# Value products of the first attention batch in two groups per pair of heads, instead of five

## Chip, cores, metric

One core of one Trainium2 chip runs the whole program. The metric is the device time of one execution in microseconds; the kernel before has a median of 1145.33 us over 3 runs (1145.01 to 1146.11).

## The reference

Four batches of attention with 8 heads, 576 positions and a head size of 64, followed by two feed-forward layers over the 4 x 576 tokens:

```python
scores = scale * np.matmul(q, k.transpose(0, 1, 3, 2))
thresh = np.max(scores, axis=-1, keepdims=True) - tau
scores = np.where(scores >= thresh, scores, -1000000000.0)
attn = np.exp(scores - np.max(scores, axis=-1, keepdims=True))
attn = attn / (np.sum(attn, axis=-1, keepdims=True) + 1e-09)
x = np.matmul(attn, v)                 # to (2304, 512)
h = x @ w_in;   x = (np.maximum(h, 0.0) + alpha * np.minimum(h, 0.0)) @ w_out
h = x @ w_in2;  y = (h * np.clip(h + 3.0, 0.0, 6.0) / 6.0) @ w_out2
```

## The kernel before

**Attention.** Heads are taken two at a time: 4 batches give 16 pairs (`pairs`, line 281), `NP` = 4 pairs to a batch. A pair has `NT` = 9 steps. Steps 0 to 7 each take 128 queries of one of the two heads, in turn; step 8 takes the last 64 queries of both heads. In a step `do_S` (line 377) makes a tile of scores on TensorE; `soft` takes its maximum on VectorE (L398), the exponential on ScalarE (L399) and the threshold with the sum on VectorE (L401). After each odd step, and after step 8, `soft_norm` divides by the sums on GpSimd (L413), `do_T` transposes the weights of both heads on TensorE (L432, L435) and ScalarE copies them to SBUF (L433, L436), and `do_PV` multiplies by the values. Beside this, `prep` gets the next pair ready in the same steps: loads on SP's queue (L296, L299), a split into a rounded part and a rest (L101 on ScalarE, L102 on GpSimd), transposes on TensorE (L322) and copies on ScalarE (L331, L342).

**The value products.** `do_T` puts the weights of steps 1 and 3 into one tile `p` of two halves, and those of steps 5 and 7 into another; there are two such buffers. Step 8 has a tile `p1` of its own. `do_PV` (lines 440 to 478) forms `pv` in PSUM, from the pool `ps_ho` of two buffers, by 5 blocks of keys for each of 2 heads, so 10 products, and a product is two matmul instructions in the trace. ScalarE copies `pv` to `xo` (L470). In the first batch (`b == 0`) this is done five times in a pair: after steps 1, 3, 5 and 7 for 128 queries, after step 8 for 64. In the other batches it is done twice: after step 3 for 256 queries, after step 8 for 256 and 64 together. After step 8 the result of the pair is split into `x0` for the feed-forward of the first batch (ScalarE L101, GpSimd L102), or stored (L476), and the last 64 rows are stored (L477). The values of the pair after next go to the buffer of this pair's (`vs`, two buffers), so their load stands on SP's queue until step 8's products are done.

**Feed-forward.** Hidden chunks of 128 (`h_group`, L216) and output groups (`o_group`, L245 and L251). The weights arrive in a 64-bit format and are decoded chunk by chunk in the first block (`decode`, L148 to L154); the first ten chunks are loaded and decoded during the first batch of attention, at steps listed in `EARLY`. The feed-forward of a block starts some steps after its attention (`LAG`), mixed into the attention of the next batch by a fixed share per step (`per`).

**Order.** The code is written in the order of the loop at line 589. A scheduler of the framework then orders the instructions of each engine by a simulated timeline, with attention raised in priority (`high_priority`); on the chip each engine runs its own list in that order.

Of the kernel before, what the change touches and what calls it, by code (L numbers as in the profile page):

```python
# [32 lines left out]
def kernel(  # L33
# [22 lines left out]
    NP = H // 2  # L56
# [43 lines left out]
    def split(hi, lo, src, lo_eng):  # L100
        nc.scalar.copy(hi, src)  # L101
        lo_eng.tensor_tensor(out=lo, in0=src, in1=f32(hi), op=ALU.subtract)  # L102
# [337 lines left out]
    def do_PV(i):  # L440
        pi, t = divmod(i, NT)
        b, hp = pairs[pi]
        vn = vs[pi % 2]
        if b == 0:
            parts = [(1, st["p"][1], 0)] if t == NT - 1 else [(2, st["p"][0], t % 4 // 2)]
        elif t in (3, NT - 1):
            parts = [(2, st["p"][0], None)] + [(1, p1, 0) for p1 in st["p"][1:]]
        else:
            return
        pv = ps_ho.tile([P, SM], F32, tag="ho", name="pv")  # L450
        at = 0
        for n, pt, u in parts:
            m = SR if n == 1 else P if u is not None else 2 * P
            for kt in range(NB + 1):
                for h in range(2):
                    blk = n * NB if kt == NB else kt + NB * h * (n - 1)
                    o = pv[64 * h:64 * h + 64, at:at + m]
                    if n == 1:
                        r = pt[:, 0, blk, SR * h:SR * h + m]
                    elif u is None:  # L460
                        o, r = o.rearrange("p (u q) -> p u q", u=2), pt[:, :, blk, :]
                    else:
                        r = pt[:, u, blk, :]
                    nc.tensor.matmul(o, lhsT=vn[:, h, kt, :], rhs=r, start=(kt == 0 and at == 0), stop=(kt == NB), skip_group_check=True)  # L464
            at += m
        if "xo" not in st[pi]:
            st[pi]["xo"] = a2.tile([P, S], F32, tag="xo", name="xo")
        xo = st[pi]["xo"]
        end = S if t == NT - 1 else t // 2 * P + P
        nc.scalar.copy(xo[:, end - at:end], pv[:, 0:at])  # L470
        if t < NT - 1:
            return
        if b == 0:
            split(x0[:, 0, hp], x0[:, 1, hp], xo[:, 0:SM], nc.gpsimd)
        else:
            nc.sync.dma_start(x1d[b][hp], xo[:, 0:SM])  # L476
        nc.sync.dma_start(x1d[rem_blk][hp, :, b * SR:(b + 1) * SR], xo[:, SM:S])  # L477
        del st[pi]
# [110 lines left out]
    for i in range(NS):  # L589
        pi, t = divmod(i, NT)  # L590
        with tc.high_priority(offset=50):
            prep(pi + 1, t)
            do_S(i)
            soft(i)
        if t % 2 == 1 or t == NT - 1:
            with tc.high_priority(offset=50):
                n = 1 + t % 2
                soft_norm(n, i)
                do_T(n, t)
                do_PV(i)  # L600
            if i in EARLY:
                if len(ws) < 7:
                    ready(*EARLY[i])
                at = early.index(EARLY[i]) + 2
                if at < len(early):
                    fetch(*early[at])
        if i % PB == PB - 1:
            emitted.add(i // PB)
        while done < min(len(queue), (i + 1 - PB - LAG) * per):
            f, a = queue[done]  # L610
            f(*a)
            done += 1
# [94 lines left out]
```

## Time and profile before

| | |
|---|---|
| Median of 3 runs | 1145.33 us |
| The profiled execution's own time | 1145.86 us |
| Its span, first to last instruction | 1144.1 us |
| TensorE, mean granted clock | 0.995 |
| TensorE busy | 1109.8 us (97%) |
| ScalarE busy | 692.4 us (61%) |
| Value products (L464), instructions | 1120 |

The engines are PE (TensorE's matmuls), PEld (its weight loads), DVE (VectorE), ACT (ScalarE), POOL (GpSimd) and SP (the queue that issues DMAs). L464 is line 464 of the kernel. A busy time is a sum over instructions and says nothing of who waits; the chain of waits goes back from the last instruction to whatever released each one.

### The profile page before, as it was taken

What the parts mean: (1) busy time and instruction counts of PE and PEld (TensorE: products, weight loads), DVE (VectorE), ACT (ScalarE), POOL (GpSimd) and SP (SyncE); (2) the same over time, 40 slices, a digit from 0 to 9 for tenths busy, and PEclk for the clock granted to TensorE, in tenths of its full rate; (3) what the DMA queues carried; (4) which work ended last, traced back from release to release, by engine and by line L of the source; (5) the groups of instructions that cost most, each with busy time, mean ns of one, the idle gap of its engine ahead of it and who ended that gap; (6) DMA issues with size and microseconds to landing.
All of it is one profiled execution on the core that took longest, in us unless ns stands there. A gap on an engine that the chain in (4) does not pass through costs nothing.

```text
span 1144.1 us, 18508 instructions
## 1 busy us (share of the span) xinstructions
PE 1109.8 (97%) x6464; PEld 913.9 (80%) x6464; DVE 611.9 (53%) x1215; ACT 692.4 (61%) x1316; POOL 681.5 (60%) x726
## 2 busy tenths in 40 slices
PE   6998999998999999999999999999999999999998
PEld 5776787877887888888878788887778888888886
DVE  6879778989897535464545535462334222232121
ACT  6989788888887565566656555565444333343332
POOL 3777779987889755556555756545334333334432
PEclk9999999999999999999999999999999999999999
DMA  5546347666775433333333522322235222222201
GB/s 166 160 130 193 115 154 228 215 217 191 223 204 191 155 107 87 106 96 107 105 101 110 151 91 63 100 72 80 84 99 172 66 65 65 61 61 65 62 31 56
DMA packets 92765, 137.44 MB, mean 120 GB/s; under 512 B 19328, under 2 KB 48512, under 8 KB 92672
## 3 DMA queue, kind: packets, MB, share of 16 engines
q1 hardware_dynamic: 92672, 136.26, 39.8%
q8 instruction: 51, 0.84, 0.3%
q14 instruction: 42, 0.34, 0.1%
HBM read 101.72 MB, written 25.17 MB: 111 GB/s over the span
## 4 chain that ended last, share of the span: by engine, by line
PE 81%; DVE 5%; ACT 4%; issue 4%; POOL 3%; DMA 2%; SPq 0%; DVEq 0%; ACTq 0%; POOLq 0%
PE h L216 32%; PE o L245 14%; PE o L251 13%; PE pv L464 7%; PE s L377 6%; PE t L432 4%; PE r L251 2%; PE r L245 2%; PE pt L322 1%; DVE nmx L398 1%; DVE e L401 1%; DMA st<-wo 1%; POOL nat L102 1%; DVE low L150 1%; POOL gs L241 1%
## 5 line engine op out<-in xcount | busy, mean ns | idle before, releaser
L216 PE MATMUL h<-x,wi 128*128 128x512 f32 (+1 forms) x1536 | 356.8, 381 | 0.0
L216 PEld LDWEIGHTS h<-x,wi 128*128 128x128 f32 x1536 | 271.9, 188 | 54.7 <-issue 1.2
L241 POOL TENSOR_TENSOR gs<-g,gs 128x512 fp32r<-128x512 f32 (+1 forms) x160 | 193.1, 1208 | 163.9 <-ACT gs L237 160.4
L251 PE MATMUL o<-wo,gs 128*128 128x512 f32 x768 | 194.8, 398 | 4.6 <-DVE g L231 2.7
L245 PE MATMUL o<-gs,wo 128*128 128x512 f32 x768 | 194.5, 397 | 0.7 <-DVE g L223 0.3
L251 PEld LDWEIGHTS o<-wo,gs 128*128 128x128 f32 x768 | 140.8, 188 | 37.8 <-DVE g L231 5.6
L245 PEld LDWEIGHTS o<-gs,wo 128*128 128x128 f32 x768 | 140.2, 188 | 30.1 <-DVE g L223 1.4
L399 ACT ACTIVATE e<-s,nmx 128x576 f32<-128x576 f32 x144 | 107.5, 750 | 48.9 <-DVE nmx L398 48.3
L231 DVE SCALAR_TENSOR_TENSOR g<-m,h 128x512 f32<-128x512 f32 x80 | 50.5, 632 | 162.0 <-ACT m L229 158.4
L401 DVE SCALAR_TENSOR_TENSOR e<-s,thr,e 128x576 f32<-128x576 f32 x144 | 116.0, 812 | 35.4 <-ACT e L399 34.8
L223 DVE SCALAR_TENSOR_TENSOR g<-m,rest_sb,h 128x512 f32<-128x512 f32 x80 | 55.3, 691 | 145.3 <-ACT m L221 134.3
L398 DVE TENSOR_REDUCE nmx<-s 128x1 f32<-128x576 f32 x144 | 106.8, 751 | 47.3 <-PE s L377 46.6
L102 POOL TENSOR_TENSOR wi<-st,wi 128x512 fp32r<-128x512 f32 x56 | 72.2, 1289 | 99.5 <-ACT wi L101 99.2
L413 POOL TENSOR_SCALAR e<-e,rc 128x576 f32<-128x576 f32 x144 | 112.5, 792 | 27.7 <-DVE rc L410 26.1
L237 ACT CAST gs<-g 128x512 fp32r<-128x512 f32 (+1 forms) x160 | 93.2, 583 | 34.6 <-DVE g L231 12.0
L229 ACT ACTIVATE m<-h,three 128x512 f32<-128x512 f32 x80 | 51.7, 648 | 102.0 <-PE h L216 102.0
L377 PE MATMUL s<-ka,qt 128*128 128x288 f32 x512 | 98.9, 320 | 6.5 <-DVE thr L400 3.7
L101 ACT CAST wo<-st 128x512 fp32r<-128x512 f32 x96 | 57.2, 620 | 78.1 <-DMA st<-wo 62.6
L221 ACT ACTIVATE m<-h 128x512 f32<-128x512 f32 x80 | 44.4, 555 | 94.0 <-PE h L216 93.5
L102 POOL TENSOR_TENSOR wo<-st,wo 128x512 fp32r<-128x512 f32 x56 | 74.3, 1344 | 41.3 <-ACT wo L101 41.3
L464 PE MATMUL pv<-p,v 128*64 128x256 f32 (+2 forms) x1120 | 97.0, 310 | 1.4 <-ACT p L433 1.1
L433 ACT COPY p<-t 128x512 f32<-128x512 f32 x144 | 82.1, 594 | 23.4 <-PE t L432 14.4
(88 smaller groups left out, 1605.0 us busy)
## 6 DMA issues: line engine op xcount, KB each, us to landing
st<-wi SPq DMA_DIRECT2D x96, 256.0 KB, 2.7
st<-wo SPq DMA_DIRECT2D x96, 256.0 KB, 2.7
raw<-in_moe_w_in_dram SPq DMA_DIRECT2D x32, 512.0 KB, 4.2
raw<-in_moe_w_out_dram SPq DMA_DIRECT2D x32, 512.0 KB, 3.9
ka<-ka SPq DMA_DIRECT2D x30, 304.0 KB, 4.4
wi<-f SPq DMA_DIRECT2D x32, 256.0 KB, 3.2
wo<-f SPq DMA_DIRECT2D x32, 256.0 KB, 3.1
raw<-in_k_dram SPq DMA_DIRECT2D x16, 256.0 KB, 3.7
```

The costliest lines, as they stand in the source:

```text
L102: lo_eng.tensor_tensor(out=lo, in0=src, in1=f32(hi), op=ALU.subtract)
L216: nc.tensor.matmul(h[:, :n], lhsT=w[:, ws, kt * P:(kt + 1) * P], rhs=x[:, xs, kt, :n], start=(i == 0), stop=(i == len(steps) - 1))
L237: nc.scalar.copy(gs[:, 0, :n], g[:, :n])
L241: nc.gpsimd.tensor_tensor(out=gs[:, 1, :n], in0=g[:, :n], in1=f32(gs[:, 0, :n]), op=ALU.subtract)
L245: nc.tensor.matmul(o[:, :n], lhsT=w[:, ws, dt * P:(dt + 1) * P], rhs=gs[:, gsel, :n], start=fresh and start and i == 0, stop=stop and i == ...
L251: nc.tensor.matmul(o[:m, :], lhsT=gs[:, gsel, tt * P:tt * P + m], rhs=w[:, ws, :], start=start and i == 0, stop=stop and i == 2)
L377: nc.tensor.matmul(ps[:, half, 0:SH], lhsT=w, rhs=s["k"][:, a, c + half * SH:c + half * SH + SH], start=(n == 0), stop=(n == len(mms) - 1))
L398: nc.vector.tensor_reduce(out=nmx, in_=ps, axis=AX.XY, op=ALU.max, negate=True)
L399: nc.scalar.activation(eh, ps, AF.Exp, bias=nmx, scale=1.0)
L401: nc.vector.scalar_tensor_tensor(out=eh, in0=ps, scalar=thr, in1=eh, op0=ALU.is_ge, op1=ALU.mult, accum_out=sm[:, h:h + 1])
L413: nc.gpsimd.tensor_scalar(out=eh, in0=eh, scalar1=rc[:, h:h + 1], scalar2=0.0, op0=ALU.mult, op1=ALU.add)
L464: nc.tensor.matmul(o, lhsT=vn[:, h, kt, :], rhs=r, start=(kt == 0 and at == 0), stop=(kt == NB), skip_group_check=True)
```

## The change

In the first batch, only the last pair of heads (`pi == NP - 1`, pair 3) keeps five groups. Pairs 0, 1 and 2 take the branch that the other batches have: nothing after steps 1, 5 and 7, 256 queries after step 3, and 256 and 64 queries in one `pv` after step 8.

```diff
@@ -441,7 +441,7 @@
         pi, t = divmod(i, NT)
         b, hp = pairs[pi]
         vn = vs[pi % 2]
-        if b == 0:
+        if pi == NP - 1:
             parts = [(1, st["p"][1], 0)] if t == NT - 1 else [(2, st["p"][0], t % 4 // 2)]
         elif t in (3, NT - 1):
             parts = [(2, st["p"][0], None)] + [(1, p1, 0) for p1 in st["p"][1:]]
```

## Rows read from the trace of the kernel before

**Rows 1.** The page: busy time of each engine over the span

```profile
PE 1109.8 (97%) x6464; PEld 913.9 (80%) x6464; DVE 611.9 (53%) x1215; ACT 692.4 (61%) x1316; POOL 681.5 (60%) x726
```

**Rows 2.** By stretch: length, PE, PEld, DVE, ACT, POOL, granted clock, DMA share, GB/s

```profile
47.06:69.73 22.67, 21.71 (x204) 17.60 (x202) 18.34 (x47) 20.25 (x45) 17.09 (x27) 1.00 0.41 118
69.73:92.40 22.67, 21.71 (x204) 17.58 (x202) 18.52 (x48) 20.96 (x46) 17.70 (x28) 1.00 0.48 139
92.40:115.40 23.00, 19.33 (x174) 15.09 (x170) 20.18 (x46) 20.84 (x42) 16.68 (x24) 0.93 0.78 223
...
122.00:400.00 278.00, 272.16 (x1554) 221.33 (x1554) 227.77 (x443) 226.12 (x415) 237.97 (x245) 0.99 0.62 193
```

**Rows 3.** Chain of waits, in order of time (start, us, what), around pair 1

```profile
46.65 1.24 PE pv L464 x18
...
57.83 1.24 PE pv L464 x18
...
60.29 0.36 PE pv L464 x2
...
61.40 0.76 DVE nmx L398
...
67.70 0.77 PE s L377 x4
```

**Rows 4.** TensorE in order of time (start, us), a group of pair 0, then pair 1

```profile
34.14 1.31 PE L464 MATMUL pv<-p,v 128*64 128x128 f32 x20
35.38 0.45 PE L322 MATMUL pt<-identr,nat 128*128 128x128 f32 x3
...
45.84 0.43 PE L464 MATMUL pv<-p,v 128*64 128x128 f32 x2
46.21 0.44 PE L322 MATMUL pt<-identr,nat 128*128 128x128 f32 x3
...
61.30 1.31 PE L464 MATMUL pv<-p,v 128*64 128x128 f32 x18
62.53 0.65 PE L432 MATMUL t<-ident,e 128*128 128x128 f32 x4
...
65.44 0.80 PE L464 MATMUL pv<-p,v 128*64 128x64 f32 x18
66.16 1.12 PE L432 MATMUL t<-ident,e 128*128 128x128 f32 x8
67.70 0.77 PE L377 MATMUL s<-ka,qt 128*128 128x288 f32 x4 [0.43 <-DVE e L401]
```

**Rows 5.** TensorE in pair 4: the 320-query group and the row after it

```profile
159.57 2.96 PE L464 MATMUL pv<-p,v 128*64 128x256 f32 x40
162.46 3.02 PE L245 MATMUL o<-gs,wo 128*128 128x512 f32 x12
```

**Rows 6.** TensorE in pair 5: the 256-query group and the row after it

```profile
190.21 2.38 PE L464 MATMUL pv<-p,v 128*64 128x256 f32 x20
192.52 0.66 PE L432 MATMUL t<-ident,e 128*128 128x128 f32 x4
```

**Rows 7.** ScalarE's copies of the products, by shape: busy us, mean ns, idle before

```profile
L470 ACT COPY xo<-pv 128x320 f32<-128x320 f32 x12 | 5.3, 439 | 5.3 <-PE pv L464 5.3
L470 ACT COPY xo<-pv 128x256 f32<-128x256 f32 x12 | 4.4, 368 | 3.8 <-PE pv L464 3.8
L470 ACT COPY xo<-pv 128x128 f32<-128x128 f32 x16 | 4.3, 269 | 0.8 <-PE pv L464 0.8
```

**Rows 8.** SP's queue in order of time (start, us)

```profile
66.14 0.39 SPq L296 DMA_DIRECT2D v<-in_v_dram  x1
```

**Rows 9.** By stretch of 2 us in pair 3, columns as in rows 2

```profile
102.00:104.00 2.00, 0.95 (x7) 0.50 (x5) 2.00 (x5) 2.00 (x4) 1.47 (x2) 1.00 0.79 252
...
106.00:108.00 2.00, 2.00 (x16) 1.25 (x12) 2.00 (x4) 2.00 (x4) 1.83 (x3) 0.55 0.47 181
108.00:110.00 2.00, 2.00 (x15) 1.43 (x13) 1.69 (x5) 1.52 (x5) 2.00 (x3) 0.60 0.77 211
```

## The prediction

> **What bounds the kernel now.** I read the page first: TensorE is busy for 97% of the span, the other engines for 53 to 61% [rows 1]. That average hides the stage which the change touches, so the second view is the busy time by stretch, cut at the pairs of the first batch [rows 2]. Pairs 1 and 2 take 22.67 us each. In both TensorE is busy for 21.71 us, ScalarE for 20.25 and 20.96, VectorE for some 18.4, GpSimd for 17 to 18: no engine is full, and two are nearly so. From 122 to 400 us, with the feed-forward mixed in, TensorE is busy for 272.16 of 278 us. So what the first batch gains or loses starts the TensorE-bound rest earlier or later by as much, as long as the decoded weights keep up; the DMA share of 0.62 in that stretch leaves them room.
>
> The third view is the chain of waits through pair 1 [rows 3]. The products after step 1 lie on it (18 instructions, 1.24 us from 46.65 us), and so do those after steps 3 (a row like it) and 5 (57.83 us). Of step 7 only the first two instructions are on it (0.36 us at 60.29 us); then the chain goes to VectorE's maximum at 61.40 us and comes back to TensorE with the scores at 67.70 us. The 64-query products of step 8 lie in that stretch and are hidden. Pair 2 repeats pair 1 nearly row by row, 22.67 us later. The fourth view is TensorE in order of time [rows 4]: a group starts with two instructions (45.84 us), another kind of work comes in until the second head's weights are copied, and then the other 18 run.
>
> **The change, part by part, for one pair.** First the price of a group. Twenty instructions for 128 queries run in 1.24 us where nothing splits them (34.14 to 35.38 us [rows 4]), 62 ns each, and in 1.61 us where the first two run alone: 0.37 us from 45.84 to 46.21 us, and 1.24 us. Twenty for 256 queries run in 2.31 us (190.21 to 192.52 us [rows 6]), and twenty for 256 with twenty for 64 in 2.89 us (159.57 to 162.46 us [rows 5]). TensorE's work for 256 queries falls from 2.48 or 3.22 to 2.31 us.
>
> The page TensorE: Matmul & The Clock Gate of the Trainium skill, section Back-to-back issue gap, speaks against the change: it gives an isolated gap of N / 2.4 + 2.5 ns, so time goes by columns and only 2.5 ns an instruction is saved. By that, an estimate, 80 instructions of 128 columns take 4.47 us and 40 of 256 take 4.37 us, a tenth of a microsecond per pair. The 62 ns of the row lie above the 56 ns of this rule and under the 81 ns which the same section gives for a stream with weight loads.
>
> Now the places, by the chain:
> - **Step 1:** its group is gone, and the scores queued behind it come 1.61 us earlier.
> - **Step 5:** the same pattern, 0.36 and 1.24 us: 1.60 us.
> - **Step 3:** 1.61 us becomes 2.31 us if it runs in one piece, or 2.67 us if its start is split off as now. I take the second, nearest to what groups do in this batch: 1.06 us more.
> - **Step 7:** the split start leaves the chain, 0.36 us less.
> - **Step 8:** its group has 256 and 64 queries. TensorE has hidden 1.23 us of step 7 (61.30 to 62.53 us) and 0.80 us of step 8 here (0.72 us for 18, so 0.80 for 20 [rows 4]); 2.89 us take their place, 0.86 more. TensorE also waits 0.43 us for VectorE before the scores at 67.70 us, so 0.43 us comes out. That holds if half of the group runs where step 7's did; its weights are ready by then. If all of it waits for step 8's weights, it is 2.89 - 0.80 - 0.43 = 1.66 us more, just ahead of the next pair's first transposes (66.16 us). These are the two ends.
> - **ScalarE's copies:** four of 0.269 us and one of 64 queries, which I bound by nothing and 0.269 us and take at 0.2, become 0.368 + 0.439 us [rows 7]: 0.27 to 0.54 us less, 0.47 taken.
> - **What is done later:** the split into `x0` (ScalarE and GpSimd) moves behind step 8's copy. Nothing reads `x0` before the feed-forward near 122 us, and GpSimd is idle for 5 us of each pair, so I cost it at nothing; without that cover it would be ScalarE and GpSimd time in the next pair's first steps. SP's queue holds the values' load until step 8's products end (issued at 66.14 us [rows 8]); behind it stand the store of the last rows and weight loads, which go out later by what step 8 ends later, up to 1.7 us. These values are for the pair after next, some 20 us away; nothing.
> - **Buffers:** half of `p` is now held from step 1 to 3, the other from 5 to 8; the next writer of either comes nearly a pair later. `ps_ho` is taken twice per pair instead of five times, which can only free it for the transposes. Nothing for both.
>
> The chain falls by 1.61 + 1.60 - 1.06 + 0.36 - 0.43 = 2.08 us, or with the bad end of step 8 by 0.85 us. But ScalarE would not follow so far: it has 20.25 - 0.47 = 19.78 us of work, and the densest pair of the batch keeps it busy for 20.96 of 22.67 us, 92.5%. At that density a pair takes 21.4 us, a gain of 1.27 us. I take 1.1 us, between 0.85 and 1.27, because ScalarE is late next: it still does exponentials and decode steps in the same order. Pairs 0, 1 and 2 have the edit: 3.3 us, with 2.6 and 6.2 us as ends. Pair 3, where ScalarE is behind with the decoding, keeps its five groups, and I count nothing there.
>
> The profiled execution took 1145.86 us, its span 1144.1 us and 1.76 us around it; less 3.3 us that is 1142.56. It lies 0.53 us above the median of 1145.33 us, so the forecast is **1142.0 us**, and its own range 1139.1 to 1142.7 us.
>
> **The rivals.** A measurement of this kernel tells about 0.2% from no change, 2.3 us.
>
> *Only the columns count* (0.27). The split starts come back in other places, the loop of scores, exponential and threshold sets the pace, and what is left is the unsplit price: 2.48 to 2.31 us, 0.17 us twice in each of three pairs, 1.0 us in all, 1144.3 us. For it: steps 7 and 8 were hidden anyway. Against it: the groups of steps 1, 3 and 5 lie on the chain at full length. A gain that is lost again at 122 us, because decoded weights come no earlier, ends here too. The page named above would end here, with still less.
>
> *Step 8 blocks the next pair* (0.11). All 40 instructions run behind step 8's weights, in front of the next pair's transposes at 66.16 us: 1.66 us lost there and 1.06 us at step 3, together 2.72 us. Steps 1, 5 and 7 give 3.57 us only if the scores behind them can start earlier; these also wait for VectorE to free their PSUM, as at 67.70 us. The case decides for slower from the point where less than 2.72 of the 3.57 us arrives. With half it is 0.93 us per pair, 2.8 us in all: 1148.1 us. Against it: the scheduler already breaks groups up for whatever is ready.
>
> *The clock falls* (0.04). In pair 3 TensorE was busy for 0.95 us of 102 to 104 us, and then its granted clock was 0.55 and 0.60 from 106 to 110 us, near the lower level of 1.2 GHz [rows 9]. That costs 2 x 0.45 + 2 x 0.40 = 1.7 us. The change takes TensorE work out of a stretch that isn't full; one fall in each of the three pairs would be 5.1 us, so with the forecast's gain 1147.1 us. Against it: pairs 1 and 2 held 1.00 at 96% busy, pair 3 had 84% [rows 2], and a pair of 21.6 us with some 1.6 us less work would have 93%. The Trainium skill, same page, section HAM oscillation, states that idle stretches between bursts bring the half clock back; this trace agrees at 106 us.
>
> *More than forecast* (0.08). All 2.08 us arrive three times, and the order around 104 us shifts so that the fall there is gone, 1.7 us: 7.9 us, 1137.4 us.
>
> That the edit does not do what it says is excluded: pairs 0 to 2 hold the same lists of `p` after steps 3 and 8 as those of later batches.
>
> **How the numbers follow.** The forecast has 0.50. Faster by over 0.2%: 0.50 + 0.08 = 0.58. Within it: 0.27. Slower: 0.11 + 0.04 = 0.15. The range of 1138.0 to 1147.2 us takes in the forecast with its bounds, the columns and the clock, and leaves out 0.19.
>
> **What would show it.** Of the value products 120 fewer instructions; pairs 1 and 2 near 21.6 us each; no value products on the chain after steps 1 and 5, a longer group after step 3; ScalarE over 91% busy there; the first feed-forward products, now from about 122 us on, some 3 us earlier. I am wrong if the pairs stay at 22.67 us (columns), if the transposes after step 8 come over 1 us later in the pair (block), if a granted clock under 1 shows before 90 us, or if the pairs gain and the end does not.

## The result, and the profile after

The change made the kernel slower: 1155.13 us is the median of 5 runs (1153.8 to 1156.5), against 1145.33 us, a ratio of 1.0085 with a 95% interval of 1.0074 to 1.0097. The profiled execution took 1156.50 us, its mean granted clock was 0.991 (0.995 before).

The page, busy time of each engine over the span:

```profile
PE 1111.5 (96%) x6344; PEld 911.3 (79%) x6344; DVE 611.8 (53%) x1215; ACT 691.9 (60%) x1307; POOL 681.5 (59%) x726
```

Against [rows 1] TensorE has 120 instructions fewer, as worked out, and no engine has more than 1.7 us more to do. The price of one instruction did not move either: a 256-query product instruction took 384 ns before and 385 after. The groups of instructions by line, engine and shape in the changed kernel (busy us, mean ns of one, idle time before):

```profile
L464 PE MATMUL pv<-p,v 128*64 128x256 f32 x600 | 76.7, 385 | 0.8 <-ACT p L433 0.5 <-DVE g L223 0.2
...
L470 ACT COPY xo<-pv 128x320 f32<-128x320 f32 x15 | 6.6, 442 | 4.4 <-PE pv L464 4.4
L470 ACT COPY xo<-pv 128x256 f32<-128x256 f32 x15 | 5.5, 369 | 3.7 <-PE pv L464 3.7
```

The copies cost 442 and 369 ns, 439 and 368 in [rows 7]. So 10 us were lost in a kernel whose work did not grow. To see where, I cut both traces at the same event of each pair: the load of the values on SP's queue, which goes out when step 8's products are done [rows 8] (in pairs 1 and 2 of the changed kernel their last four instructions run just behind it, at 70.29 and 96.97 us). SP's queue of the changed kernel in order of time:

```profile
44.86 0.79 SPq L296 DMA_DIRECT2D v<-in_v_dram  x1
...
124.31 0.38 SPq L296 DMA_DIRECT2D v<-in_v_dram  x1
```

In the changed kernel these loads go out at 44.86, 69.13, 96.50 and 124.31 us; before, they were at 44.17, 66.14, 88.81 and 114.80 us. Pair 0 lost 0.7 us, pair 1 2.3, pair 2 4.7, pair 3, whose products have no edit, 1.8: 9.5 of the 10.6 us by which the span grew (1144.1 to 1154.7 us). The busy time by stretch with these cuts (columns as in rows 2), pairs 1 to 3, first before:

```profile
44.17:66.14 21.97, 21.43 (x202) 17.59 (x200) 17.43 (x46) 19.61 (x44) 17.10 (x26) 1.00 0.45 137
66.14:88.81 22.67, 21.71 (x202) 17.59 (x200) 18.48 (x48) 20.25 (x44) 17.50 (x27) 1.00 0.48 139
88.81:114.80 25.99, 22.42 (x198) 17.55 (x196) 23.18 (x53) 23.83 (x49) 18.93 (x28) 0.93 0.74 212
```

and after:

```profile
44.86:69.13 24.27, 21.30 (x144) 15.62 (x143) 18.40 (x46) 18.18 (x36) 17.58 (x27) 0.93 0.49 140
69.13:96.50 27.37, 23.08 (x165) 17.73 (x166) 18.33 (x44) 20.57 (x41) 16.86 (x26) 0.88 0.36 101
96.50:124.31 27.81, 22.77 (x200) 18.22 (x200) 25.23 (x60) 24.59 (x49) 20.30 (x29) 0.94 0.61 193
```

In pairs 1 and 2 TensorE stands idle for 24.27 - 21.30 = 2.97 and 4.29 us, against 0.54 and 0.96. ScalarE, which I had expected to be next in line, is busy for 75% in both. And the granted clock is no longer 1.00. By stretches of 2 us, at the two seams between pairs:

```profile
48.00:50.00 2.00, 0.59 (x3) 0.59 (x4) 1.90 (x6) 1.37 (x2) 2.00 (x3) 0.86 0.92 174
50.00:52.00 2.00, 2.00 (x12) 1.99 (x10) 1.05 (x3) 0.59 (x1) 1.69 (x4) 0.50 0.72 191
52.00:54.00 2.00, 2.00 (x13) 1.72 (x11) 2.00 (x7) 1.69 (x3) 1.47 (x2) 0.78 0.24 93
...
72.00:74.00 2.00, 0.37 (x1) 0.38 (x2) 1.30 (x5) 2.00 (x6) 1.50 (x3) 0.84 0.46 155
74.00:76.00 2.00, 0.95 (x4) 0.61 (x3) 1.06 (x3) 1.25 (x3) 2.00 (x2) 0.50 0.80 161
76.00:78.00 2.00, 1.85 (x8) 1.86 (x9) 1.44 (x5) 1.11 (x2) 2.00 (x3) 0.50 0.92 268
78.00:80.00 2.00, 2.00 (x10) 1.80 (x9) 1.60 (x4) 1.35 (x3) 1.26 (x5) 0.50 0.14 36
```

TensorE does little for 2 us (0.59 us from 48 us on, 0.37 from 72), then its clock is granted at half, its lower level of 1.2 GHz. Busy time times the missing share of the clock is 0.08 + 1.00 + 0.44 = 1.5 us at the first fall and, with the slice from 80 us, 2.5 us at the second. That splits the losses: pair 1 has 2.43 us more idle, 1.5 us of slow clock and 1.65 us less work inside its cuts, 2.3 in all; pair 2 has 3.33, 2.5 and 1.2 less, 4.7 in all. **In these two pairs the loss is TensorE waiting, and its lower clock.**

The work that is missing inside the cuts is, in pair 1, not that of the value products. Counted from the start of each piece of products to the start of what follows it on TensorE, or to its own end, the products take 7.15, 7.45 and 7.45 us in pairs 0, 1 and 2 before, and 6.64, 7.44 and 6.79 us after. So 1.2 us are saved in three pairs, and nothing in pair 1, because the joined groups are broken up as the narrow ones were. The group after step 3 of pair 1, TensorE in order of time:

```profile
53.72 0.65 PE L464 MATMUL pv<-p,v 128*64 128x256 f32 x2
54.30 0.44 PE L322 MATMUL pt<-identr,nat 128*128 128x128 f32 x3
...
55.13 1.94 PE L464 MATMUL pv<-p,v 128*64 128x256 f32 x14
57.00 0.66 PE L432 MATMUL t<-ident,e 128*128 128x128 f32 x4
57.59 0.65 PE L464 MATMUL pv<-p,v 128*64 128x256 f32 x4
58.17 0.46 PE L322 MATMUL pt<-identr,nat 128*128 128x128 f32 x3
```

Its pieces of 2, 14 and 4 instructions take 0.58 + 1.87 + 0.58 = 3.03 us, where 20 in one piece took 2.31 [rows 6]. Step 8's group comes in seven pieces (from 60.95, 63.25, 66.21, 67.48, 68.07, 68.65 and 70.29 us) and takes 4.4 us, where 40 in one piece took 2.89 [rows 5]. What left pair 1's stretch is other work, which now stands on the other side of a cut: 12 transposes by L322 instead of 18, and 36 instructions of scores instead of 40.

What TensorE waits for at the seam of pairs 1 and 2, its instructions in order of time:

```profile
68.65 0.45 PE L464 MATMUL pv<-p,v 128*64 128x64 f32 x6
69.03 0.65 PE L432 MATMUL t<-ident,e 128*128 128x128 f32 x4
...
73.63 1.33 PE L377 MATMUL s<-ka,qt 128*128 128x288 f32 x4 [1.78 <-DVE e L401]
76.15 1.11 PE L432 MATMUL t<-ident,e 128*128 128x128 f32 x4 [1.19 <-POOL e L413]
```

and ScalarE, after and then before at the same seam:

```profile
67.00 0.74 ACT L399 ACTIVATE e<-s,nmx 128x576 f32<-128x576 f32 x1 [0.42 <-DVE nmx L398]
69.77 0.58 ACT L433 COPY p<-t 128x512 f32<-128x512 f32 x1 [2.03 <-PE t L432]
70.25 0.49 ACT L331 CAST ka<-pt 128x384 fp32r<-128x384 f32 x1
70.62 0.61 ACT L433 COPY p<-t 128x512 f32<-128x512 f32 x1
71.10 0.46 ACT L470 COPY xo<-pv 128x320 f32<-128x320 f32 x1
71.42 0.65 ACT L101 CAST wo<-f 128x512 fp32r<-128x512 f32 x1
71.94 0.77 ACT L399 ACTIVATE e<-s,nmx 128x576 f32<-128x576 f32 x1
```

```profile
65.92 0.75 ACT L399 ACTIVATE e<-s,nmx 128x576 f32<-128x576 f32 x1
66.55 0.21 ACT L470 COPY xo<-pv 128x64 f32<-128x64 f32 x1
66.64 0.77 ACT L399 ACTIVATE e<-s,nmx 128x576 f32<-128x576 f32 x1
67.28 1.10 ACT L433 COPY p<-t 128x512 f32<-128x512 f32 x2
```

Read it like this. ScalarE's list now has the copies of transposed weights ahead of the next exponential. The transposes stand on TensorE behind step 8's products, so ScalarE waits 2.03 us for them. The exponential's own maximum comes only at the end of that wait, at 69.68 us (the trace has `nmx` from 68.93, 0.75 us); its scores ran in three pieces between those products, the last at 68.32 us. Then five instructions stand ahead of it in ScalarE's list, from 69.77 us on: two copies of weights, a copy of keys, the copy of `pv` and a cast of decoded weights. So the exponential runs at 71.94, 2.26 us after its maximum, VectorE's threshold follows it, and TensorE waits 1.78 us for the PSUM of those scores. Before, two exponentials ran first and the copies after them, without a wait.

The waits by engine and line (total us, times, longest), pairs 1 and 2, before and after:

```profile
DVE nmx L398 <- PE s L377: 6.2, 8, 1.8
```

```profile
DVE nmx L398 <- PE s L377: 9.9, 10, 2.0
ACT p L433 <- PE t L432: 6.3, 5, 2.0
```

Before, no wait of ScalarE's copies for transposes is among the seven largest. At the seam of pairs 0 and 1 another piece of the list does it. The chain of waits after:

```profile
47.35 1.28 POOL x L102
48.63 0.73 POOL e L413
...
49.41 1.11 PE t L432 x4
```

The split into `x0`, now possible only after step 8, stands on GpSimd ahead of the normalisation for which the transposes of 49.41 us wait.

### The profile page after: what moved, and what is told of

Same layout as the page of the kernel before. It is cut to its first block, busy times and chain, and to the rows that moved or that the text cites. A ratio compares the mean times of both kernels' runs of the same rounds, so it can differ in the third digit from the quotient of the medians.

```text
span 1154.7 us, 18281 instructions
## 1 busy us (share of the span) xinstructions
PE 1111.5 (96%) x6344; PEld 911.3 (79%) x6344; DVE 611.8 (53%) x1215; ACT 691.9 (60%) x1307; POOL 681.5 (59%) x726
## 4 chain that ended last, share of the span: by engine, by line
PE 76%; ACT 8%; DVE 5%; issue 4%; POOL 4%; DMA 3%; SPq 0%; DVEq 0%; ACTq 0%; POOLq 0%
PE h L216 30%; PE o L245 13%; PE o L251 12%; PE pv L464 6%; PE s L377 6%; PE t L432 4%; PE r L251 2%; PE r L245 2%; DMA wi<-f 1%; ACT e L399 1%; PE pt L322 1%; ACT low L148 1%; ACT p L433 1%; POOL wo L102 1%; DVE nmx L398 1%
## 5 line engine op out<-in xcount | busy, mean ns | idle before, releaser
L432 PE MATMUL t<-ident,e 128*128 128x128 f32 x576 | 90.0, 283 | 8.1 <-POOL e L413 4.7
```

What stands on the lines that cost most here:

```text
L432: nc.tensor.transpose(ps[:, kt], e[:, c:c + P], ident)
```

## The experiments

The instructions of every engine are put in order by the framework's scheduler, so each edit below changes more than its own lines. All ratios have 95% intervals; the kernel before had medians of 1145.2 to 1145.7 us beside these runs. The last column is the load that goes out after pair 3's step 8 (114.80 us before, 124.31 after).

| run | us | ratio | pairs 1, 2, 3 (us) | end of batch 1 |
|---|---|---|---|---|
| before | 1145.33 | | 21.97, 22.67, 25.99 | 114.80 |
| after | 1155.13 | 1.0085 [1.0074, 1.0097] | 24.27, 27.37, 27.81 | 124.31 |
| e1 | 1152.9 | 1.0067 [1.0050, 1.0083] | 25.76, 23.59, 24.10 | 119.40 |
| e2 | 1147.6 | 1.0016 [1.0007, 1.0025] | 23.28, 24.39, 22.75 | 115.22 |
| e3 | 1150.96 | 1.0048 [1.0033, 1.0063] | 22.81, 20.91, 28.10 | 116.37 |
| e4 | 1154.53 | 1.0082 [1.0059, 1.0106] | 24.23, 27.38, 27.80 | 124.44 |
| e5 | 1146.47 | 1.0011 [1.0002, 1.0021] | 22.72, 21.68, 25.28 | 114.99 |
| e6 | 1154.15 | 1.0080 [1.0064, 1.0095] | 22.61, 25.99, 26.42 | 120.66 |
| e7 | 1154.65 | 1.0084 [1.0067, 1.0101] | 25.14, 21.06, 25.53 | 120.83 |
| e8 | 1155.76 | 1.0089 [1.0074, 1.0104] | 23.47, 28.12, 28.83 | 126.03 |
| e9 | 1146.4 | 1.0012 [1.0002, 1.0021] | 22.12, 22.52, 23.26 | 115.37 |
| e10 | 1145.94 | 1.0006 [0.9996, 1.0015] | 20.84, 26.03, 25.49 | 116.15 |
| e11 | 1161.2 | 1.0144 [1.0129, 1.0159] | 22.67, 27.36, 27.78 | 122.67 |
| e12 | 1157.72 | 1.0108 [1.0091, 1.0126] | 25.94, 28.47, 22.55 | 122.94 |
| e13 | 1156.22 | 1.0100 [1.0085, 1.0115] | 27.40, 24.75, 24.14 | 122.21 |
| e14 | 1149.0 | 1.0030 [1.0019, 1.0041] | 21.93, 23.25, 25.29 | 118.74 |
| e15 | 1147.89 | 1.0027 [1.0015, 1.0040] | 21.81, 22.64, 26.94 | 116.58 |
| e16 | 1149.18 | 1.0036 [1.0024, 1.0049] | 23.31, 25.31, 24.26 | 116.41 |
| e17 | 1149.65 | 1.0044 [1.0030, 1.0057] | 24.33, 25.24, 25.00 | 118.62 |
| e18 | 1157.21 | 1.0101 [1.0084, 1.0118] | 24.62, 26.30, 30.13 | 125.91 |

**Which group costs it (e1 to e3).** Each has a part of the change's grouping in pairs 0 to 2: e1 has 256, 256 and 64 queries after steps 3, 7 and 8; e2 keeps 128 after 1 and 3 and joins the rest; e3 joins only the first half.

```diff
+        elif b == 0 and t in (3, 7, NT - 1):        # e1
+            parts = [(1, st["p"][1], 0)] if t == NT - 1 else [(2, st["p"][0], None)]
+        elif b == 0 and t in (1, 3):                # e2
+            parts = [(2, st["p"][0], t % 4 // 2)]
+        elif b == 0 and t in (5, 7, NT - 1):        # e3
+            parts = [(1, st["p"][1], 0)] if t == NT - 1 else [(2, st["p"][0], t % 4 // 2)]
         elif t in (3, NT - 1):
```

> Groups after steps 3, 7 and 8 (256, 256 and 64 queries): the same 256-query groups as the change, but none stands behind step 8's weights and the split into x0 need not wait for the long group. Theory 'step 8 blocks the next pair': the loss is at the seam of two pairs, so this run is near the kernel before or a little under it, 1143 to 1147 us, and TensorE's waits at the seams and the fall of the granted clock there are gone. Rival 'any long group blocks': 256-query groups hold up the scores wherever they stand, 1152 to 1156 us.

> Groups after steps 1 and 3 as before, and one of 256 and 64 queries after step 8. Theory 'step 8 blocks': all of the loss stays, 1152 to 1156 us. Rival 'any long group blocks': half of the loss, near 1150 us. Rival 'the split into x0 on GpSimd': 1152 to 1156 us too.

> One group of 256 queries after step 3, then groups after steps 5, 7 and 8 as before. Theory 'step 8 blocks': no loss, 1143 to 1146 us. Rival 'any long group blocks': half of the loss, near 1150 us.

The joined group of step 8 does not explain the loss: with it alone (e2) 1.9 us are lost, without it (e1, e3) 7.2 and 5.3. The 1.9 us are a flattering figure, though: e2 loses 3.0 us in pairs 1 and 2, and its pair 3 is 3.2 us shorter than before, with the clock at 1.00 where the kernel before has 0.93. Of the three, the two that join steps 1 and 3 lose the most.

**The split into x0 (e4, e18).** e4 writes the split of pairs 0 to 2 behind step 4 of the next pair:

```diff
-        if b == 0:
+        if b == 0 and pi < NP - 1:
+            late[(pi + 1) * NT + 4] = hp, xo
+        elif b == 0:
             split(x0[:, 0, hp], x0[:, 1, hp], xo[:, 0:SM], nc.gpsimd)
```

> The change as it is, with the split into x0 of pairs 0 to 2 moved into step 4 of the next pair. Rival 'the split into x0 on GpSimd': the 1.3 us of GpSimd ahead of the next pair's normalisation and what follows from it are the loss, so 1146 to 1149 us. Theory 'step 8 blocks on TensorE': the split is one of several late arrivals, and only some 1.3 us in each of two or three seams comes back, 1151 to 1154 us.

Nothing changed, but this run decides nothing: its trace has the split at 47.52 us, still ahead of the normalisation, so the place in the code did not move it. e18 ties it down by a dependence on step 5 of the next pair:

```diff
+            if i in late:                           # (pi + 1) * NT + 5
+                hp, xo = late.pop(i)
+                for half in range(2):
+                    nc.gpsimd.tensor_scalar(out=x0[:, half, hp, 0:2], in0=st["e"][1], scalar1=0.0, scalar2=0.0, op0=ALU.mult, op1=ALU.mult)
+                split(x0[:, 0, hp], x0[:, 1, hp], xo[:, 0:SM], nc.gpsimd)
```

> The change, with the split into x0 of pairs 0 to 2 tied to step 5 of the next pair (two small GpSimd instructions per pair, 0.2 us each, write two columns of x0 from that step's sums, and are overwritten; the split has to follow them). In the run that moved the split in the code alone it stayed where it was, at 47.52 us on GpSimd in front of the normalisation that the transposes of 49.58 us waited for, so that run did not decide. Theory A (the late split is the cause of what pair 1 loses): the normalisation comes 1.3 us earlier, TensorE does not wait 1.4 us near 49 us, the clock stays 1.00 there, pair 1 takes 22.0 us or less and the whole 1151 us or less. Theory B (GpSimd's list fills the same place with another instruction, here the 1.28 us of a weight's split, and the pairs are set by the order as a whole): the wait near 49 us stays over 1 us, pair 1 takes 22.5 us or more and the whole 1153 us or more.

GpSimd in e18, in order of time:

```profile
47.55 1.27 POOL L102 TENSOR_TENSOR wi<-f,wi 128x512 fp32r<-128x512 f32 x1 [0.45 <-ACT wi L101]
48.79 1.47 POOL L413 TENSOR_SCALAR e<-e,rc 128x576 f32<-128x576 f32 x2
```

Theory B: a decoded weight's split took the place, the normalisation starts at 48.79 us (48.60 in the change), the clock falls at 50 us as it did, pair 1 takes 24.62 us. The wait is real, but `x0` is only what happened to stand there.

**Held PSUM, late products, priority (e5, e6, e8).** e5 keeps the change's places and one PSUM tile from step 1 to 3, but with instructions of 128 queries. e6 takes the products out of the raised priority. e8 runs 6 of the 10 products after steps 3 and 7 and 4 a step later.

```diff
+        if pi < NP - 1:                             # e5
+            parts = [(n, pt, u) for n, pt, v in parts for u in ((0, 1) if v is None else (v,))]
...
+            if pi < NP - 1:                         # e6, outside the block of high priority
                 do_PV(i)
...
+            kts = range(NB + 1)                     # e8
+            if spread and n == 2:
+                kts = range(3) if first else range(3, NB + 1)
```

> The change's places with the old instructions: in pairs 0 to 2 every product is 128 queries wide again (100 instructions a pair, as before), but issued after steps 3 and 8 only. Theory 'late and long': what costs is that value products come late in long runs, in front of scores that a steady flow needs, so this is as slow as the change or slower, 1153 to 1158 us. Rival 'the wide instruction itself': near the kernel before, 1145 to 1148 us.

> The change with the value products of pairs 0 to 2 issued at ordinary priority, so that ready scores and transposes may go in front of them. Theory 'late and long': half or more of the loss comes back, 1145 to 1150 us. Rival 'the products must be done early because something waits for their result or their buffer': no gain or worse, 1154 to 1160 us.

> The change's wide products, but each group of 256 queries in two halves: six of ten products after steps 3 and 7, the other four after step 4's scores and with step 8's 64 queries. Theory 'late and long': runs of half the length, so a good part of the loss comes back, 1146 to 1150 us. Rival 'fewer groups in any form' (what counts is how many steps pass without products): 1152 to 1156 us.

e5 did not place the products late: each half ran as soon as its own weights were there (step 1's twenty instructions start at 46.89 and 48.42 us, step 3's at 52.88 and 54.50). It shows that a longer hold of PSUM costs little (1.0 us in all) and leaves "late" open. e6 is slow by 8.7 us with a granted clock of 1.00 through pairs 1 and 2, so a fall there is not needed for the loss. Shorter runs of products (e8) do not help.

**The clock (e7).** Ten constant products ahead of the first transposes of pairs 1 and 2; this kernel does more work than the change.

```diff
+            if t == 1 and h == 0 and st["pi"] in (1, 2):
+                for _ in range(10):
+                    nc.tensor.matmul(ps[:, 0], lhsT=ident, rhs=ident, start=True, stop=True)
...
```

> The change with ten extra products of constants (20 instructions, some 1.2 us) on TensorE ahead of the first transposes of pairs 1 and 2, where it stands idle and the granted clock falls. Rival 'the clock': the falls near 50 and 74 us go, and some 4 us with them, 1149 to 1152 us. Theory 'late and long': the fall follows from the waits, which stay; 1153 to 1157 us.

The falls at 50 and 74 us are gone, the time is not back. The order changed too (pair 0 took 4.9 us longer than before, pair 2 21.06 us), so this bounds the clock only loosely; e11 below prices a fall better.

**Is it waiting for the later weights? (e9, e12).** Both keep the change's groups and halve each instruction to 64 queries of either step's half, so that none can start before the later step's weights are copied. e9 does all 10 products for the first 64 queries and then all for the other 64; e12 does the two instructions of a product back to back.

```diff
+        if pi < NP - 1:                             # e9
+            parts = [(n, pt, u, c) for n, pt, u in parts for c in ((0, 1) if u is None else (None,))]
...
+                        if c is not None:
+                            o, r = o[:, :, 64 * c:64 * c + 64], r[:, :, 64 * c:64 * c + 64]
...
+                    if pi < NP - 1 and u is None and n == 2:      # e12
+                        for c in range(2):
+                            nc.tensor.matmul(o[:, :, 64 * c:64 * c + 64], lhsT=vn[:, h, kt, :], rhs=r[:, :, 64 * c:64 * c + 64],
+                                             start=(kt == 0 and at == 0 and c == 0), stop=(kt == NB), skip_group_check=True)
+                        continue
```

> The change's groups with 128-query instructions (100 a pair, as before), but each takes 64 queries of step 1 (or 5) and 64 of step 3 (or 7), so that none can run before the later step's weights. In the run with late five groups, the products of steps 1 and 5 ran early, as soon as their own weights were there. Theory 'what waits': the products of the earlier step can no longer fill TensorE's gaps and come in a heap after the later one, so this is as slow as the change or slower by the columns' price, 1153 to 1158 us. Rival 'the wide instruction': near the kernel before, 1145 to 1148 us.

> The change with every 256-query product replaced in its place by two of 128 (64 queries of each half), so that TensorE's order begins as in the change and its work is that of the kernel before. Theory 'order': slow wherever the order is the change's, 1150 to 1157 us. Rival 'the wide product itself': 1145 to 1148 us, like the earlier run with narrow pieces.

Pairs 1 and 2 by stretch, e9 and then e12 (columns as in rows 2):

```profile
47.47:69.59 22.12, 18.81 (x196) 15.98 (x192) 18.27 (x45) 18.93 (x39) 16.22 (x25) 1.00 0.43 117
69.59:92.11 22.52, 20.40 (x201) 16.61 (x197) 18.86 (x47) 19.39 (x40) 17.42 (x26) 1.00 0.46 136
```

```profile
45.98:71.92 25.94, 23.25 (x210) 18.77 (x212) 19.38 (x47) 21.71 (x43) 19.23 (x28) 1.00 0.43 123
71.92:100.39 28.47, 24.88 (x201) 19.68 (x201) 21.03 (x51) 19.89 (x40) 16.89 (x26) 0.94 0.37 109
```

This pair of runs is the clearest of the study. The two kernels have the same instructions with the same sizes, and their products wait for the same data. Only the sequence in which they are written differs, and they are 1157.72 - 1146.40 = 11.3 us apart. So neither the join nor the wait for the later weights costs 10 us by itself. e12 also clears the 256-query instruction: without it the loss is as large. A part of the difference is again how the products are broken up: in pairs 1 and 2 they take 6.42 and 6.27 us of TensorE in 7 and 6 pieces in e9, and 7.70 and 8.77 us in 11 and 14 pieces in e12, 3.8 of the 9.8 us by which these two pairs differ. The total of e9 hides a loss as that of e2 does: pair 0 ends 3.3 us later than before, and pair 3 is 2.7 us shorter, with the clock at 1.00.

**Order alone (e10, e11, e13, e15).** e10 and e15 are small edits of the kernel before: step 7's products in step 8's PSUM tile, and the second head's products first. e13 is e15's edit on the change. e11 is the change with the raised priority set to 46 instead of 50, which adds or takes away no instruction.

```diff
+            if t == 7 and pi < NP - 1:              # e10
+                return
...
+            if t == NT - 1 and pi < NP - 1:
+                parts = [(2, st["p"][0], 1)] + parts
...
-                for h in range(2):                  # e13, e15
+                for h in ((1, 0) if pi < NP - 1 else (0, 1)):
...
-        with tc.high_priority(offset=50):           # e11, both places
+        with tc.high_priority(offset=46):
```

> The kernel before with step 7's products put into step 8's PSUM tile in pairs 0 to 2: the same matmuls, free to run when they are ready, one copy less, and another order on all engines from pair 0 on. Theory 'what waits': nothing waits longer, so 1144 to 1147.5 us. Rival 'any new order of the first batch costs': slower by 3 us or more, 1148 to 1156 us.

> The change with the attention's priority raised by 46 places instead of 50: the order of the first batch is that of the change, and only the order behind some 125 us differs. It measures what a new order of the later part is worth. Theory 'what waits': the loss sits in the first batch, so 1152 to 1157 us. Rival 'the loss is made behind the first batch': it moves by more than 4 us.

> The change with the two heads' products in the other sequence within a group (head 1 first) in pairs 0 to 2: same instructions, another order. Theory 'order': moves by 3 us or more against the change in either direction, anywhere from 1144 to 1162 us. Rival 'the wide product itself': 1152 to 1157 us.

> The kernel before with head 1's products first in pairs 0 to 2, narrow as they are. Theory 'order' taken to its end (any order of the first batch may cost): 1144 to 1156 us, so off the kernel before by 3 us or more with good chance. Rival 'narrow products lead to good orders because they fill gaps': 1144 to 1148 us, like the four narrow kernels so far.

The heads' sequence costs the kernel before 2.5 us. The change moves by 1.1 us, which is within the intervals of the two ratios and less than the 3 us expected, though its pair 1 is 3.1 us longer and its pairs 2 and 3 are 2.6 and 3.7 us shorter. e10 is even in all, but its pairs 1 and 2 take 20.84 and 26.03 us: single pairs move by several us on edits that do nothing. e11 has the change's order on every engine up to some 125 us, and yet pair 1 is 1.6 us shorter. By stretch:

```profile
44.86:67.53 22.67, 19.71 (x144) 14.07 (x143) 18.43 (x46) 18.24 (x36) 17.49 (x27) 1.00 0.52 150
...
48.00:50.00 2.00, 0.61 (x5) 0.61 (x6) 1.90 (x6) 1.39 (x2) 2.00 (x3) 1.00 0.88 170
50.00:52.00 2.00, 2.00 (x18) 1.92 (x16) 1.71 (x6) 1.19 (x2) 1.80 (x5) 1.00 0.72 220
```

Here the clock does not fall after the same gap. That prices one fall at 24.27 - 22.67 = 1.6 us, and it shows the rest of pair 1: TensorE is busy for 19.71 us and idle for 2.96, just as in the change. So with a full clock the pair is still 0.7 us longer than before, with 1.7 us less work inside its cuts, none of which is saved in the value products (7.44 us, as in the change). Yet e11 ends 6 us later than the change, all of it from the order after the first batch.

**The change elsewhere (e14, e16, e17).** e14 issues the joined groups one step later, behind the next scores; e16 does so in pairs 1 and 2 only; e17 makes the change in pairs 1 and 2 only.

```diff
+            if held:                                # e14, behind the next step's scores
+                now = st["p"]
+                st["p"] = held[0]
+                do_PV(held[1])
+                st["p"] = now
+                held = None
...
+                if pi >= NP - 1:
+                    do_PV(i)
+                else:
+                    held = [st["p"], i]
...
-        if pi == NP - 1:                            # e16, e17
+        if pi in (0, NP - 1):
```

> The change with its two groups issued one step later (behind the next step's scores and softmax, still in attention's priority). Theory 'order': another order, so the time moves by 3 us or more against the change, 1144 to 1162 us. Rival 'the wide product itself': 1152 to 1157 us.

> Two wide groups, issued one step later, in pairs 1 and 2 alone; pair 0 keeps its five. Theory 'order': pair 0 ends near 44 us, pairs 1 and 2 take 22 to 23 us each, and the whole is 1143.5 to 1147 us; a gain of the columns' price, under 1 us, may show. Rival 'the wide product itself': two thirds of the loss, 1150 us or more.

> The change in pairs 1 and 2 alone, issued where the change has them. Theory 'order': not to be told beforehand, 1145 to 1155 us. Rival 'every pair with wide groups costs its share': pairs 1 and 2 cost 2 to 5 us each as in the change, 1150 to 1154 us.

Pairs 1 and 2 of e14 by stretch:

```profile
48.27:70.20 21.93, 19.54 (x151) 14.30 (x150) 18.66 (x48) 18.93 (x39) 17.26 (x26) 1.00 0.47 135
70.20:93.45 23.25, 20.84 (x161) 15.17 (x161) 17.46 (x43) 19.70 (x41) 16.37 (x25) 1.00 0.43 119
```

With the products out of the way of the next scores, pairs 1 and 2 are back within 0.6 us of before; pair 0 lost 4.1 us instead. The value products took 6.95 and 6.64 us of TensorE in these two pairs, 0.5 and 0.8 less than before, and the pairs did not become shorter by that. e16 missed both of its forecasts: pair 0 ends at 43.53 us, but pairs 1 and 2 take 23.31 and 25.31 us, and the whole is 3.9 us slower. e17's mean clock is 1.000 and it is still slower by 4.4 us. No run beat the kernel before.

## Why the prediction was wrong

**The step that failed** is the first term of the sum: "its group is gone, and the scores queued behind it come 1.61 us earlier", and the same 1.60 us for step 5, against only 1.06 us more at step 3. It took a piece out of the chain of waits and moved the rest up. Three things were wrong with that.

The first is shown, and it is a price. By the sum, the products of a pair would take 2.67 + 2.89 = 5.56 us of TensorE instead of 7.45. They took 6.64, 7.44 and 6.79 us in pairs 0 to 2: the prices came from groups that ran unbroken or were split once, and the joined groups ran in 6, 10 and 7 pieces. What was gone after steps 1 and 5 came back after steps 3 and 8.

The second is shown too, and it is a term that the sum lacked: new idle time of TensorE. The sum even took 0.43 us of waiting out. Idle time rose from 0.54 to 2.97 us in pair 1 and from 0.96 to 4.29 in pair 2. It does not need the lower clock: in e6, e9, e11 and e14, whose clock held in pair 1, TensorE is idle there for 3.25, 3.31, 2.96 and 2.39 us, and the pair takes 21.93 to 22.67 us, where it took 21.97. No single engine is full in them either. As I read it, the pair is held by the loop of scores, maximum, exponential, threshold, normalisation and transposes in the order in which the engines' lists have them, and the value products on the chain had filled time in which that loop waited; no run tests this reading by itself.

The third is that the rest of the order did not stay. My text before the prediction names the scheduler, the sum gave it no price, and the pairs without an edit in that place (pair 3: 1.8 us) paid as well.

**Point by point.**
- *120 instructions fewer, prices of single instructions and copies:* right, to a few ns. ScalarE's copies of products take 1.5 us less in all, where 0.47 us for each of three pairs was worked out; it did not matter. The prices of the groups were not right: 3.03 and 4.4 us in pair 1, for 2.67 and 2.89.
- *The gain per pair, 1.1 us for pairs 0 to 2:* measured +0.7, +2.3 and +4.7 us.
- *ScalarE as the next limit, over 91% busy:* 75%.
- *The split into `x0` at no cost, "without that cover it would be ScalarE and GpSimd time in the next pair's first steps":* it came to stand there, 1.28 us on the chain. GpSimd's 5 idle us of a pair were no cover, because idle time elsewhere doesn't help a list that is served in order. e18 shows that taking it away brings nothing.
- *Only the columns count:* wrong in size. Of its reasons, that the split starts come back in other places is what the pieces show; that the loop sets the pace fits the runs and is not shown.
- *Step 8 blocks the next pair:* the right sign, and the waits do lie at that seam, with copies and exponentials behind step 8's transposes. But e1 and e3 lose without that group, and e2 loses 3.0 us in pairs 1 and 2 with it, where the change loses 7.0.
- *The clock falls:* two of the three falls came, 1.6 us for the one that can be compared (1.7 forecast), some 2.5 us by the windows for the other. With 0.04 I had this too low; it is up to 4 of the 7 us lost in pairs 1 and 2. The falls come behind stretches in which TensorE does little, and the loss does not need them: e6 and e17 lose 8.7 and 4.4 us with the clock at 1.00 there.
- *What would show me wrong:* a granted clock under 1 came at 50 us, the pairs went above 22.67 us, and the first feed-forward products, meant to come 3 us earlier than 122 us, start at 131.4 us.

**What is open.** That the sequence decides is shown by e9 against e12 and by e11. Which property of the sequence makes a list bad is not. A wait of ScalarE's copies for transposes is large in the change (6.3 us) and in e12 (6.2), and not among the largest waits of e9; but e6 is slow with 2.8 us of it. I could not take one wait out of the changed kernel and leave the rest of its order as it was: every edit of the products gave a new order.

## What to carry to other kernels

Before you price an edit by a row on the chain, ask what the chain would wait for without it: if no engine of that stage is full, shorter work there can become idle time, as in e14. Price a joined group by the pieces in which it will run, not by an unbroken group of another stage: here 20 instructions took 2.31 us in one piece and 3.03 in three. Where a scheduler orders all engines, make two or three edits that do nothing (a swapped loop, another priority) and see how far they move the time: here 0.6 to 6 us, so a sum of 3 us from single rows could not be trusted in either direction. Cut both traces at one event of every stage, and compare length, busy time and clock stage by stage, before you look for a cause.

## What the runs showed of the hardware

The clock does not follow from the length of a gap alone. In the change TensorE waited 1.43 us before 49.41 us and 1.78 us before 73.63 us, and its clock fell to 0.50 after both. In e11 the same gap, with 0.61 us of work in that stretch of 2 us, left it at 1.00. In e6 TensorE was busy for only 0.20 us of the stretch from 72 to 74 us, and the clock stayed at 1.00 too. So it did after two gaps in e9, TensorE in order of time:

```profile
49.78 1.37 PE L432 MATMUL t<-ident,e 128*128 128x128 f32 x8 [1.45 <-POOL e L413]
...
61.15 0.66 PE L432 MATMUL t<-ident,e 128*128 128x128 f32 x4 [1.79 <-POOL e L413]
```

The Trainium skill, page TensorE: Matmul & The Clock Gate, section HAM oscillation, states that idle stretches between bursts bring the half clock back. The change agrees at 50 and 74 us; e6, e9 and e11 show that such a stretch need not do so, and no run here shows what decides.
